# Attention, experts and SwiGLU in one kernel: the order of the first expert's choice, of one weight conversion and of two small tables, and a last tile in halves

## The chip, the cores and the metric

The kernel runs on one core of a Trainium2 chip. The metric is the device time of one launch in microseconds (us), as the median of several runs. A difference of 0.2% is 2.2 us here.

## The reference

Three layers run one after the other on random data:

```python
attn = 1 / (1 + exp(-(q @ k.T / sqrt(64) - log(448))))       # q, k, v: 4 batches, 12 heads, 448 x 64
x    = (attn @ v) as [1792 tokens, 768]
e    = argmax(x @ w_gate)                                     # 8 experts
x    = gate_w * (relu(x @ w1[e]) @ w2[e])                     # 768 -> 1024 -> 768, gate_w a softmax weight
out  = (silu(x @ w2_gate) * (x @ w2_val)) @ w2_out            # 768 -> 1536 -> 768, 64-bit weights
```

## The kernel before

**Attention** walks over 24 pairs of heads, 4 batches of 6 pairs, in a loop written out by hand (`for i, (b, g) in enumerate(pairs)`, from L449). Inside `tc.manual_schedule()` the instructions of every engine stand in the order in which the code issues them, so a line of Python that stands later is queued later on each engine. In iteration i TensorE (PE) computes the scores of pair i+1 in four chunks (`scores`, L214), transposes k and q of pair i+2 (`transpose_qk`, L202), multiplies pair i with v (`av`, L229) and folds pair i-1 (`fold`, L249: it transposes the result back and adds the gate logits of that pair). ScalarE (ACT) makes the sigmoids of the chunks (L226), whose PSUM buffers are two. `load` (L181) fetches q, k and v of pair i+4 on the queue of SyncE (SP).

**Conversion.** The SwiGLU weights are 64-bit numbers. `load_r64` (L137) fetches a block of them, 768 KB, and `convert` (L147) builds 32-bit numbers from their bits in three steps: s0 with one ACT instruction (L152) and one of VectorE (DVE, L153), s1 with one of DVE (L157), s2 with one of DVE (L161) and two of GpSimd (POOL, L163 and L164). One block is converted per pair, its steps between the chunks of the scores, and is stored on POOL's queue (L431). The scratch tile `u` has one buffer.

**Routing.** For each batch, once its six folds are done, a list `tail` gives work to the folds that follow, one item per fold: `gate` (L288), `ranks` with `places` (L300 and L329), and for the third batch also `choose_first` with `first_slot` (L345 and L363), which guess the expert that most tokens chose, and `first_perm` (L379), which finds 128 of its tokens and gathers their rows of x from DRAM (L390). These rows, transposed by `first_x` (L395), meet the guessed expert's weights in `first_product` (L404) while the table of all slots is still being made. The weights of the guess are loaded from L133, w1 in six blocks of 512 KB and w2 in eight of 384 KB.

**The slot table** (L560 to L598) is a run of small DVE instructions. It gives each slot of 128 tokens its expert (`slot_e`), a mark for a new expert (`slot_n`) and its row in the result (`slot_c`). After it the gate weights of the slots, `gsl`, are added up from a PSUM tile `pg` (L596 to L598).

**Experts** (from L907): 19 slots, each with transposed rows, two products, the weights split in a high and a low part (`split_w`, L758). The first matmuls of the stage are transposes into a new PSUM tile (L909), then products with w2 (L921).

**SwiGLU**: `gemm1` (L673) over 12 blocks of columns and four pieces of tokens, then 14 output tiles (L1035 to L1056), each of 72 matmuls into a PSUM tile of two banks, a copy by ACT (L1052) and an indirect store by POOL (L1053) to the tokens' rows.

Of the kernel before, what the change touches and what calls it, by code (L numbers as in the profile page):

```python
# [9 lines left out]
F32 = mybir.dt.float32  # L10
F32R = mybir.dt.float32r
BF16 = mybir.dt.bfloat16
I32 = mybir.dt.int32
U32 = mybir.dt.uint32
AF = mybir.ActivationFunctionType
ALU = mybir.AluOpType
# [6 lines left out]
def sigmoid_attention_moe_swiglu_kernel(  # L23
# [13 lines left out]
    nc = tc.nc  # L37
    B, H, S, D = q.shape
    NT, DM = out.shape
# [3 lines left out]
    P = 128  # L43
# [5 lines left out]
    K2 = F2 // P  # L49
    HH = H // 2  # L50
    HW = DM // 2
    NT_P = NT // P
    NS = (NT + E * (P - 1)) // P
    NSP = NS + (NS % 2)
# [37 lines left out]
    perm_c = const.tile([P, NT_P], I32, name="perm_c")  # L92
# [9 lines left out]
    gsl = const.tile([P, NSP], F32, name="gsl")  # L102
# [65 lines left out]
    with ExitStack() as actx:  # L168
# [12 lines left out]
        def load(nm, i):  # L181
            b, g = pairs[i]
            src = {"q": q, "k": k, "v": v}[nm][b, 2 * g:2 * g + 2]
            if nm == "v":
                t = qkv.tile([CP, 2, C, D], F32, tag=nm, name="vraw", bufs=5)
                nc.sync.dma_start(t, src.rearrange("h (p c) d -> p h c d", c=C))
            else:
                t = qkv.tile([CP, C, 2, D], F32, tag=nm, name=nm + "raw", bufs=4)
                for h in range(2):
                    nc.sync.dma_start(t[:, :, h], src[h].rearrange("(p c) d -> p c d", c=C))  # L190
            raw[nm, i] = t
# [5 lines left out]
        n = len(pairs)  # L197
# [31 lines left out]
        def av(i):  # L229
            vt = raw.pop(("v", i))  # L230
            a = am.pop(i)
            pu = ps_u.tile([P, 512], F32, tag="u", name="pu")
            for c in range(C):
                for h in range(2):
                    nc.tensor.matmul(pu[h * D:(h + 1) * D, :S], vt[:, h, c], a[:, c, h],  # L235
                                     start=(c == 0), stop=(c == C - 1))
            u = up.tile([P, S], F32, tag="u", name="u")
            nc.vector.tensor_copy(u, pu[:, :S])  # L238
            us[i] = u
            qk.pop(("q", i))  # L240
            qk.pop(("k", i))
# [172 lines left out]
        with tc.manual_schedule():  # L414
# [1 line left out]
                for nm in "kqv":  # L416
                    load(nm, i)
            nc.sync.dma_start(fwt[:, :, P:], w_gate.rearrange("(g p) e -> p g e", p=P))
            for i in (2, 3):
                for nm in "kqv":  # L420
                    load(nm, i)
            conv = {}
            cvw = {}

            def load_conv(i):
                r = cvp.tile([P, DM * 2], I32, tag="r64", name="r64", bufs=2)
                load_r64(r, ("gv"[i // K2], i % K2))
                conv[i] = r

            def store_conv(i):  # L430
                nc.gpsimd.dma_start(wgd[i], cvw.pop(i))  # L431

            load_conv(0)
            load_conv(1)
            pw = ps_u.tile([P, 512], F32, tag="u", name="pw")

# [12 lines left out]
            for i, (b, g) in enumerate(pairs):  # L449
                if i + 1 < n:  # L450
                    scores(i + 1, 0)
                    scores(i + 1, 1)
                cvw[i] = cvp.tile([P, DM], F32, tag="w", name="w", bufs=2)
                cv = convert(conv.pop(i), cvp.tile([P, DM], I32, tag="u", name="u", bufs=1),
                             cvw[i])
                if i + 2 < n:
                    transpose_qk(i + 2)
                cv[0]()
                if i + 4 < n:
                    for nm in "kqv":  # L460
                        load(nm, i + 4)
                if i + 1 < n:
                    scores(i + 1, 2)
                    scores(i + 1, 3)
                cv[1]()
                cv[2]()
                store_conv(i)
                if i + 2 < n:
                    load_conv(i + 2)
                av(i)  # L470
                if i > 0:
                    fold(i - 1, tail.pop(0) if tail else None)
                if i == n - 1:
                    first_x()
                if g == 0 and b > 0:
                    tail.append(lambda px, b=b: lambda: gate(b - 1))

                    def rank_place(px, b=b):
                        evac = ranks(b - 1, px)

                        def done():
                            evac()
                            places(b - 1)
                        return done

                    tail.append(rank_place)
                    if b == B - 1:
                        tail.append(lambda px: lambda: (choose_first(B - 2), first_slot()))
                        tail.append(first_perm)
                if i == n - 2:  # L490
                    ge = nc.values_load(guess[0:1, 0:1], engines=[SP], min_val=0, max_val=E - 1,
                                        skip_runtime_bounds_check_because=why)
                    for j in range(KD):
                        load_w(0, j, ge)
                elif i == n - 1:
                    for j in range(3):
                        load_w(1, j, ge)
# [70 lines left out]
            for t in range(T):  # L568
# [5 lines left out]
            se = rp.tile([P, NS, E], F32, tag="se", name="se")  # L574
            V.tensor_tensor(se, iota_s[:, :NS, None].to_broadcast([P, NS, E]),
                            cum.to_broadcast([P, NS, E]), op=ALU.is_ge)
            sf = rp.tile([P, NS], F32, tag="sf", name="sf")
            V.tensor_reduce(sf, se, axis=AX.X, op=ALU.add)
            V.tensor_scalar(sf, sf, float(E - 1), gf, op0=ALU.min, op1=ALU.add)
# [13 lines left out]
            V.tensor_add(sf, sf, iota_p[:, :NS])  # L593
            V.tensor_scalar(slot_c, sf, float(NT), None, op0=ALU.min)

            V.tensor_copy(gsl, pg[:, :NSP])  # L596
            for i in (1, 2):
                V.tensor_add(gsl, pg[:, i * NSP:(i + 1) * NSP], gsl)  # L598

    ectx = ExitStack()  # L600
    early = ectx.enter_context(tc.tile_pool(name="early", bufs=2, side="right", reuse_waits="tile"))
# [297 lines left out]
    with tc.manual_schedule():  # L899
# [135 lines left out]
        for t in range(NT_P):  # L1035
            po = ps_a.tile([P, 2, 512], F32, tag="a", name="po")
            hh, hl = hs.pop(t)
            for f in range(K2):
                for st, mv, i in ((hh, 0, 0), (hh, 1, 1), (hl, 0, 2)):
                    for m in range(2):  # L1040
                        nc.tensor.matmul(po[:, m, :HW], st[:, f],  # L1041
                                         wo[f][mv][:, m * HW:(m + 1) * HW],
                                         start=(f == 0 and i == 0),
                                         stop=(f == K2 - 1 and i == 2))
            if t + 2 < NT_P:
                split_h(t + 2)
                for f in range(KS, K2):
                    split_hb(t + 2, f)
                if t + 3 < NT_P:
                    load_h(t + 3)  # L1050
            ob = post.tile([P, DM], F32, tag="ob", name="ob", bufs=2)
            nc.scalar.copy(ob.rearrange("p (m f) -> p m f", m=2), po[:, :, :HW])  # L1052
            nc.gpsimd.indirect_dma_start(  # L1053
                out=out[:, :],
                out_offset=bass.IndirectOffsetOnAxis(ap=perm_c[:, t:t + 1], axis=0),
                in_=ob[:, :], in_offset=None)  # L1056
# [31 lines left out]
```

## Time and profile before

| | |
|---|---|
| median of 3 runs | 1124.3 us (1124.15 to 1124.78) |
| the profiled execution | 1125.06 us, span 1123.5 us |
| TensorE (PE) | 1093.8 us busy, 97% of the span |
| VectorE (DVE) | 627.9 us, 56% |
| ScalarE (ACT) | 531.7 us, 47% |
| GpSimd (POOL) | 277.1 us, 25% |
| DMA | 168.17 MB, mean 150 GB/s |

The profiled execution took 1.56 us more than its span and 0.76 us more than the median. In the lists of the profile an instruction is named by its line, engine, operation and tiles; a bracket behind it tells how long its engine sat idle before it and what ended that. PE is busy nearly throughout, so what counts is where it is idle and what clock it was granted (a clock of 1.00 is 2.4 GHz, 0.50 is 1.2 GHz).

### The profile page before, as it was taken

To read this page: it belongs to the slowest core of one execution; us is meant where nothing else is said; L and a number is where in the kernel's file an instruction comes from. 1 tells how busy PE (TensorE), PEld (TensorE's weight loads), DVE (VectorE), ACT (ScalarE), POOL (GpSimd) and SP (SyncE) were. 2 spreads that over 40 slices of the span, in tenths; PEclk is the share of its full clock that TensorE was granted. 3 is DMA by queue.
4 is the path that set the end of the run, shared out by engine and by line. 5 is a ranking of instruction groups with operands and counts; after the bars stand their busy time and mean duration, and the time that the engine had idled before them with its cause. 6 is when DMAs were issued, how large, how long until landed. Compare 5 with 4: busy or idle time off the path is not lost. (4 is left out here: it accounts for less than half of the span.)

```text
span 1123.5 us, 16847 instructions
## 1 busy us (share of the span) xinstructions
PE 1093.8 (97%) x6130; PEld 913.7 (81%) x6130; DVE 627.9 (56%) x918; ACT 531.7 (47%) x720; POOL 277.1 (25%) x241
## 2 busy tenths in 40 slices
PE   7999999789999999999999999999999999999996
PEld 5565655468989798989888888888888889999996
DVE  3667777569899999999954333333333335111210
ACT  5666676248889788888852211111111124111210
POOL 2555556422222422223101011111111110000100
PEclk9999999889999999999999999999999999999998
DMA  8898987722445883644322232222222324322220
GB/s 208 240 272 247 273 250 214 282 99 85 159 152 183 299 321 125 214 153 169 127 96 99 86 112 103 104 103 103 104 104 104 113 94 137 105 83 76 75 89 29
DMA packets 124278, 168.17 MB, mean 150 GB/s; under 512 B 50592, under 2 KB 94112, under 8 KB 124192
## 3 DMA queue, kind: packets, MB, share of 16 engines
q1 hardware_dynamic: 118112, 137.16, 38.3%
q0 software_dynamic: 6080, 29.90, 7.3%
q8 instruction: 50, 0.82, 0.3%
q14 instruction: 36, 0.29, 0.1%
HBM read 195.98 MB, written 41.82 MB: 212 GB/s over the span
## 5 line engine op out<-in xcount | busy, mean ns | idle before, releaser
L687 PE MATMUL psf<-y,wgh 128*128 128x512 f32 (+1 forms) x1152 | 322.9, 367 | 0.2 <-ACTq L944 0.2
L765 DVE TENSOR_TENSOR wlo<-wraw,whi 128x768 fp32r<-128x768 f32 (+1 forms) x256 | 271.1, 1108 | 29.3 <-ACT whi L763 27.6
L763 ACT CAST whi<-wraw 128x768 fp32r<-128x768 f32 (+1 forms) x256 | 230.2, 929 | 51.7 <-PE hps L787 32.4
L687 PEld LDWEIGHTS psf<-y,wgh 128*128 128x128 f32 x1152 | 205.1, 188 | 36.6 <-ACTq L944 0.5
L687 PE MATMUL psf<-y,wgl 128*128 128x512 f32 (+1 forms) x576 | 210.5, 365 | 0.0
L163 POOL TENSOR_SCALAR w<-w 128x768 f32<-128x768 f32 x36 | 84.7, 2354 | 312.3 <-ACT w L152 312.3
L692 ACT ACTIVATE sg<-psf 128x512 f32<-128x512 f32 (+1 forms) x48 | 26.1, 544 | 250.0 <-PE psf L687 250.0
L1041 PE MATMUL po<-y,hh 128*128 128x384 f32 x672 | 144.1, 335 | 0.0
L693 DVE TENSOR_TENSOR sg<-psf,sg 128x512 f32<-128x512 f32 (+1 forms) x48 | 30.0, 625 | 194.6 <-ACT sg L692 194.6
L687 PEld LDWEIGHTS psf<-y,wgl 128*128 128x128 f32 x576 | 108.3, 188 | 18.8
L226 ACT ACTIVATE a<-sc,logs 112x896 f32<-112x896 f32 x96 | 91.9, 1015 | 58.9 <-PE sc L224 58.7
L1041 PEld LDWEIGHTS po<-y,hh 128*128 128x128 f32 x672 | 119.3, 188 | 0.0
L75 DVE TENSOR_TENSOR hl<-ht,hh 128x1280 fp32r<-128x1280 f32 x14 | 20.9, 1491 | 125.1 <-ACT hh L74 125.1
L1041 PE MATMUL po<-y,hl 128*128 128x384 f32 x336 | 85.6, 335 | 0.0
L235 PE MATMUL pu<-a,vraw 112*64 112x448 f32 x384 | 77.5, 545 | 0.4 <-DVE u L238 0.4
L787 PE MATMUL yps<-whi,hh 128*128 128x384 f32 x296 | 77.2, 341 | 0.0
L787 PE MATMUL yps<-wlo,hh 128*128 128x384 f32 x296 | 75.9, 337 | 0.8 <-DVE wlo L765 0.8
L787 PE MATMUL yps<-whi,hl 128*128 128x384 f32 x296 | 75.4, 335 | 0.0
L74 ACT CAST hh<-ht 128x1280 fp32r<-128x1280 f32 x14 | 17.7, 1265 | 120.0 <-PE po L1041 120.0
L164 POOL TENSOR_TENSOR w<-w,u 128x768 f32<-128x768 f32 x36 | 66.6, 1849 | 29.6 <-DVE u L161 29.3
L787 PE MATMUL hps<-whi,xh 128*128 128x512 f32 x216 | 68.4, 397 | 0.0
L787 PE MATMUL hps<-wlo,xh 128*128 128x512 f32 x216 | 67.3, 393 | 1.1 <-DVE wlo L765 1.1
(189 smaller groups left out, 1494.8 us busy)
## 6 DMA issues: line engine op xcount, KB each, us to landing
wraw<-in_moe_w_dram SPq DMA_DIRECT2D x148, 384.0 KB
wraw<-in_moe_w_dram SPq DMA_DIRECT2D x108, 512.0 KB
r<-in_moe_w_gate_dram SPq DMA_DIRECT2D x12, 768.0 KB
wgd<-w POOLq DMA_DIRECT2D x24, 384.0 KB, 5.6
r<-in_moe_w_val_dram SPq DMA_DIRECT2D x12, 768.0 KB
w<-wgd SPq DMA_DIRECT2D x24, 384.0 KB
r<-in_moe_w_out_dram SPq DMA_DIRECT2D x12, 768.0 KB
ht<-hd SPq DMA_DIRECT2D x14, 640.0 KB
```

The costliest lines, as they stand in the source:

```text
L75: nc.vector.tensor_sub(lo, src, hi.bitcast(F32))
L163: nc.gpsimd.tensor_scalar(w, w, TINY, None, op0=ALU.is_ge)
L164: nc.gpsimd.tensor_tensor(w, w, u.bitcast(F32), op=ALU.mult)
L226: nc.scalar.activation(am[i][:, c], sc[:CP, :, :S], AF.Sigmoid, bias=logs[:CP], scale=SCALE)
L235: nc.tensor.matmul(pu[h * D:(h + 1) * D, :S], vt[:, h, c], a[:, c, h], start=(c == 0), stop=(c == C - 1))
L687: nc.tensor.matmul(ps[:, i, :cn], st[:, a], mv[:, j, :cn], start=(j == 0 and m == 0), stop=(j == KD - 1 and m == 2))
L692: nc.scalar.activation(sg[:, :cn], ps[:, 0, :cn], AF.Sigmoid)
L693: nc.vector.tensor_mul(sg[:, :cn], ps[:, 0, :cn], sg[:, :cn])
L763: nc.scalar.copy(hi[:, :w], r)
L765: nc.vector.tensor_sub(lo[:, :w0], r[:, :w0], hi[:, :w0].bitcast(F32))
L787: nc.tensor.matmul(ps[:, m, :w], st[:, a], mv[:, m * w:(m + 1) * w], start=(j == 0 and i == 0), stop=(j == m_ - 1 and i == 2))
L1041: nc.tensor.matmul(po[:, m, :HW], st[:, f], wo[f][mv][:, m * HW:(m + 1) * HW], start=(f == 0 and i == 0), stop=(f == K2 - 1 and i == 2))
```

## The change

Five moves. (1) `load_conv(0)` stands ahead of the loads of pair 3 instead of behind them. (2) In iteration 0 the whole conversion stands behind `av(0)`; in the others it stays where it was. In all of them `load_conv(i + 2)` stands behind `av(i)`; it issues on SP alone, where `av` has nothing. (3) The items of `tail` are appended ahead of the fold of the same iteration, so each item runs with the fold before the one it ran with. (4) `gsl` is added up ahead of the rest of the slot table. (5) The last output tile is computed column half by column half; each half is copied and stored by itself, with indices `perm_h` into rows of half length.

```diff
@@ -416,9 +416,8 @@
                 for nm in "kqv":
                     load(nm, i)
             nc.sync.dma_start(fwt[:, :, P:], w_gate.rearrange("(g p) e -> p g e", p=P))
-            for i in (2, 3):
-                for nm in "kqv":
-                    load(nm, i)
+            for nm in "kqv":
+                load(nm, 2)
             conv = {}
             cvw = {}
 
@@ -431,6 +430,8 @@
                 nc.gpsimd.dma_start(wgd[i], cvw.pop(i))
 
             load_conv(0)
+            for nm in "kqv":
+                load(nm, 3)
             load_conv(1)
             pw = ps_u.tile([P, 512], F32, tag="u", name="pw")
 
@@ -455,38 +456,44 @@
                              cvw[i])
                 if i + 2 < n:
                     transpose_qk(i + 2)
-                cv[0]()
+                if i > 0:
+                    cv[0]()
                 if i + 4 < n:
                     for nm in "kqv":
                         load(nm, i + 4)
                 if i + 1 < n:
                     scores(i + 1, 2)
                     scores(i + 1, 3)
-                cv[1]()
-                cv[2]()
-                store_conv(i)
+                if i > 0:
+                    cv[1]()
+                    cv[2]()
+                    store_conv(i)
+                av(i)
+                if i == 0:
+                    for f in cv:
+                        f()
+                    store_conv(i)
                 if i + 2 < n:
                     load_conv(i + 2)
-                av(i)
+                if g == 0 and b > 0:
+                    tail.append(lambda px, b=b: lambda: gate(b - 1))
+
+                    def rank_place(px, b=b):
+                        evac = ranks(b - 1, px)
+
+                        def done():
+                            evac()
+                            places(b - 1)
+                        return done
+
+                    tail.append(rank_place)
+                    if b == B - 1:
+                        tail.append(lambda px: lambda: (choose_first(B - 2), first_slot()))
+                        tail.append(first_perm)
                 if i > 0:
                     fold(i - 1, tail.pop(0) if tail else None)
                 if i == n - 1:
                     first_x()
-                if g == 0 and b > 0:
-                    tail.append(lambda px, b=b: lambda: gate(b - 1))
-
-                    def rank_place(px, b=b):
-                        evac = ranks(b - 1, px)
-
-                        def done():
-                            evac()
-                            places(b - 1)
-                        return done
-
-                    tail.append(rank_place)
-                    if b == B - 1:
-                        tail.append(lambda px: lambda: (choose_first(B - 2), first_slot()))
-                        tail.append(first_perm)
                 if i == n - 2:
                     ge = nc.values_load(guess[0:1, 0:1], engines=[SP], min_val=0, max_val=E - 1,
                                         skip_runtime_bounds_check_because=why)
@@ -574,6 +581,9 @@
             se = rp.tile([P, NS, E], F32, tag="se", name="se")
             V.tensor_tensor(se, iota_s[:, :NS, None].to_broadcast([P, NS, E]),
                             cum.to_broadcast([P, NS, E]), op=ALU.is_ge)
+            V.tensor_copy(gsl, pg[:, :NSP])
+            for i in (1, 2):
+                V.tensor_add(gsl, pg[:, i * NSP:(i + 1) * NSP], gsl)
             sf = rp.tile([P, NS], F32, tag="sf", name="sf")
             V.tensor_reduce(sf, se, axis=AX.X, op=ALU.add)
             V.tensor_scalar(sf, sf, float(E - 1), gf, op0=ALU.min, op1=ALU.add)
@@ -593,9 +603,6 @@
             V.tensor_add(sf, sf, iota_p[:, :NS])
             V.tensor_scalar(slot_c, sf, float(NT), None, op0=ALU.min)
 
-            V.tensor_copy(gsl, pg[:, :NSP])
-            for i in (1, 2):
-                V.tensor_add(gsl, pg[:, i * NSP:(i + 1) * NSP], gsl)
 
     ectx = ExitStack()
     early = ectx.enter_context(tc.tile_pool(name="early", bufs=2, side="right", reuse_waits="tile"))
@@ -1035,13 +1042,29 @@
         for t in range(NT_P):
             po = ps_a.tile([P, 2, 512], F32, tag="a", name="po")
             hh, hl = hs.pop(t)
-            for f in range(K2):
-                for st, mv, i in ((hh, 0, 0), (hh, 1, 1), (hl, 0, 2)):
-                    for m in range(2):
-                        nc.tensor.matmul(po[:, m, :HW], st[:, f],
-                                         wo[f][mv][:, m * HW:(m + 1) * HW],
-                                         start=(f == 0 and i == 0),
-                                         stop=(f == K2 - 1 and i == 2))
+            last = t == NT_P - 1
+            order = [(f, x, m) for f in range(K2) for x in range(3) for m in range(2)]
+            if last:
+                order.sort(key=lambda a: a[2])
+                ob = post.tile([P, DM], F32, tag="ob", name="ob", bufs=2)
+            for f, x, m in order:
+                st, mv = ((hh, 0), (hh, 1), (hl, 0))[x]
+                nc.tensor.matmul(po[:, m, :HW], st[:, f], wo[f][mv][:, m * HW:(m + 1) * HW],
+                                 start=(f == 0 and x == 0), stop=(f == K2 - 1 and x == 2))
+                if last and f == K2 - 1 and x == 2:
+                    ms = slice(m * HW, (m + 1) * HW)
+                    nc.scalar.copy(ob[:, ms], po[:, m, :HW])
+                    nc.gpsimd.indirect_dma_start(
+                        out=out.rearrange("n (h c) -> (n h) c", h=2),
+                        out_offset=bass.IndirectOffsetOnAxis(ap=perm_h[:, m:m + 1], axis=0),
+                        in_=ob[:, ms], in_offset=None)
+            if last:
+                break
+            if t == 0:
+                perm_h = post.tile([P, 2], I32, tag="permh", name="permh", bufs=1)
+                for m in range(2):
+                    nc.vector.tensor_scalar(perm_h[:, m:m + 1], perm_c[:, NT_P - 1:], 1, m,
+                                            op0=ALU.logical_shift_left, op1=ALU.bitwise_or)
             if t + 2 < NT_P:
                 split_h(t + 2)
                 for f in range(KS, K2):
```

On ACT, at the start (`a_307` the sigmoids of pair 1, `a_388` those of pair 2, `qh` the high part of q, `w_324` of the first conversion). Before, and then now:

```order
L74 CAST qh_340<-pq_335 128x448
L152 ACTIVATE w_324<-r64_184 128x768
L226 ACTIVATE a_307<-sc_354,logs_72 112x896
L226 ACTIVATE a_307<-sc_362,logs_72 112x896
L226 ACTIVATE a_388<-sc_389,logs_72 112x896
```

```order
L74 CAST qh_340<-pq_335 128x448
L226 ACTIVATE a_307<-sc_352,logs_72 112x896
L226 ACTIVATE a_307<-sc_360,logs_72 112x896
L152 ACTIVATE w_324<-r64_176 128x768
L226 ACTIVATE a_388<-sc_389,logs_72 112x896
```

The conversion's ACT instruction stood ahead of the last two sigmoids of pair 1; it now stands behind them.

On POOL, at the end of attention (`wgd` is where a converted block is stored, `rot` to `oh0` belong to the choice of the first slot, `x0` is its gather). Before, and then now:

```order
L431 DMA wgd_64<-w_2330 128x768
L353 TENSOR_SCALAR rot_147<-iota_e_91,gf_86 128x8
...
L375 TENSOR_TENSOR oh0_2416<-tok2_101,z_2411 112x24
L163 TENSOR_SCALAR w_2435<-w_2435 128x768
...
L431 DMA wgd_64<-w_2435 128x768
L390 DMA x0_2497<-xd_60,perm0_85 128x768
L163 TENSOR_SCALAR w_2508<-w_2508 128x768
...
L431 DMA wgd_64<-w_2508 128x768
L716 DMA xg_2740<-xd_60,perm_g_76 128x768
```

```order
L430 DMA wgd_64<-w_2247 128x768
L353 TENSOR_SCALAR rot_147<-iota_e_91,gf_86 128x8
...
L375 TENSOR_TENSOR oh0_2333<-tok2_101,z_2328 112x24
L163 TENSOR_SCALAR w_2352<-w_2352 128x768
...
L430 DMA wgd_64<-w_2352 128x768
L390 DMA x0_2433<-xd_60,perm0_85 128x768
L163 TENSOR_SCALAR w_2452<-w_2452 128x768
...
L163 TENSOR_SCALAR w_2508<-w_2508 128x768
...
L723 DMA xg_2740<-xd_60,perm_g_76 128x768
```

The choice and the gather each stand one conversion earlier: two conversions now follow the gather ahead of `xg`, where one did.

On DVE, the slot table (`se`, `sf` the sums of which it is made, `pg` the PSUM tile of the gate weights). Before, and then now:

```order
L575 TENSOR_TENSOR se<-iota_s,cum 128x168
L578 TENSOR_REDUCE sf<-se 128x21
...
L594 TENSOR_SCALAR slot_c<-sf 128x21
L596 COPY gsl<-pg 128x22
L598 TENSOR_TENSOR gsl<-pg,gsl 128x22 x2
```

```order
L582 TENSOR_TENSOR se<-iota_s,cum 128x168
L584 COPY gsl<-pg 128x22
L586 TENSOR_TENSOR gsl<-pg,gsl 128x22 x2
L588 TENSOR_REDUCE sf<-se 128x21
...
L604 TENSOR_SCALAR slot_c<-sf 128x21
```

The last reads of `pg` now stand ahead of 13 instructions of the table instead of behind them.

## Rows read from the trace of the kernel before

**Rows 1.** Windows: us, busy us by engine (instructions), PEclk, DMA share, GB/s.

```profile
60.00:200.00 140.00, 139.38 (x988) 81.47 (x988) 103.74 (x223) 94.72 (x124) 83.09 (x61) 1.00 0.87 251
...
300.00:590.00 290.00, 287.54 (x1553) 260.85 (x1553) 262.77 (x286) 244.60 (x316) 74.36 (x84) 1.00 0.54 185
```

**Rows 2.** Waits, engine PE: total us, times, longest us.

```profile
PE pt L400 <- DMA x<-xd,perm: 7.2, 1, 7.2
...
PE pt L909 <- DVE gsl L598: 3.2, 1, 3.2
```

**Rows 3.** Timeline of PE, first pairs: start us, us, instructions [idle before].

```profile
16.83 3.23 PE L235 MATMUL pu<-a,vraw 112*64 112x448 f32 x16
23.10 0.46 PE L224 MATMUL sc<-qh,kh 64*112 64x448 f32 x2 [3.04 <-ACT a L226]
```

**Rows 4.** Timeline of ACT, the same stretch.

```profile
21.24 0.91 ACT L152 ACTIVATE w<-r 128x768 f32<-128x768 f32 x1 [4.75 <-DMA r<-in_moe_w_gate_dram]
22.06 4.00 ACT L226 ACTIVATE a<-sc,logs 112x896 f32<-112x896 f32 x4
```

**Rows 5.** Timeline of PE, from the last fold but one to the experts.

```profile
205.97 1.18 PE L259 MATMUL px<-fwt,u 128*112 128x136 f32 x8
214.31 1.51 PE L400 MATMUL pt<-ident,x 128*128 128x128 f32 x6 [7.17 <-DMA x<-xd,perm]
...
217.70 2.59 PE L408 MATMUL hps<-wraw,x0t 128*128 128x512 f32 x4
...
220.44 7.11 PE L408 MATMUL hps<-wraw,x0t 128*128 128x512 f32 x16
...
229.89 0.72 PE L569 MATMUL pg<-oh,ohl 112*128 112x66 bf16 x16
233.80 1.94 PE L909 MATMUL pt<-ident,hsb 128*128 128x128 f32 x8 [3.18 <-DVE gsl L598]
```

**Rows 6.** Windows, columns as in the first group: where the clock was low.

```profile
24.00:28.00 4.00, 4.00 (x22) 3.03 (x24) 2.15 (x5) 3.71 (x5) 3.41 (x3) 0.57 0.93 255
...
208.00:212.00 4.00, 0.00 (x0) 0.00 (x0) 0.89 (x5) 0.00 (x0) 3.62 (x3) 1.00 0.93 336
214.30:220.00 5.70, 5.68 (x18) 4.04 (x19) 1.86 (x9) 2.55 (x4) 0.00 (x0) 0.58 0.98 383
233.80:240.00 6.20, 6.20 (x16) 4.03 (x17) 3.51 (x5) 4.10 (x6) 0.00 (x0) 0.53 0.07 30
```

**Rows 7.** Timeline of POOL, end of attention.

```profile
195.73 0.59 POOL L431 DMA_DIRECT2D wgd<-w  x1 [0.30 <-POOL w L164]
...
205.93 1.22 POOL L390 DMA_INDIRECT x<-xd,perm  x1 [0.40 <-issue]
```

**Rows 8.** Tiles x and xg: gathers from issue to landing.

```profile
DMA to landing us min/median/max: 8.2/8.2/8.2
...
DMA to landing us min/median/max: 3.8/4.1/4.6
```

**Rows 9.** Timeline of SP's queue, the loads of the guessed expert.

```profile
203.44 0.58 SPq L278 DMA_DIRECT2D xd<-xt  x1
205.41 7.33 SPq L133 DMA_DIRECT2D wraw<-in_moe_w_dram  x9
```

**Rows 10.** Timeline of DVE, last fold but one and end of the slot table.

```profile
208.40 0.16 DVE L268 COPY lp<-px 112x8 f32<-112x8 f32 x1
...
230.31 0.33 DVE L578 TENSOR_REDUCE sf<-se 128x21 f32<-128x168 f32 x1
...
233.25 0.40 DVE L598 TENSOR_TENSOR gsl<-pg,gsl 128x22 f32<-128x22 f32 x2
```

**Rows 11.** The last store: its copy, a half-width copy elsewhere, GB/s by 0.2 us.

```profile
1114.30 0.80 ACT L1052 COPY ob<-po 128x768 f32<-128x768 f32 x1 [11.75 <-PE po L1041]
...
L402 ACT COPY x0t<-pt x2: 479/479/479, 215.2 to 215.9; 128x384 f32<-128x384 f32 x2
...
GB/s 0 0 0 0 0 0 0 0 0 399 307 307 461 461 31 0 0 0 0 0 0 0 0 0 0 0 0 0 0 0 0 0 0 0 0 0 0 0 0 0
```

More of the change, by code (lines that the diff above doesn't have):

```diff
@@ L464, in sigmoid_attention_moe_swiglu_kernel @@
                     scores(i + 1, 3)
-                cv[1]()
-                cv[2]()
-                store_conv(i)
+                if i > 0:
[7 more added lines that the diff above has]
+                    store_conv(i)
                 if i + 2 < n:
                     load_conv(i + 2)
-                av(i)
[L471 to L474, printed above, removed]
                 if g == 0 and b > 0:
@@ L489, in sigmoid_attention_moe_swiglu_kernel @@
                         tail.append(first_perm)
+                if i > 0:
+                    fold(i - 1, tail.pop(0) if tail else None)
+                if i == n - 1:
+                    first_x()
                 if i == n - 2:
```

## The prediction, before the changed kernel was run

> **What bounds the kernel now.** I read the windows first. PE is busy for 139.38 of the 140 us of steady attention and for 287.54 of 290 us of the experts [rows 1], at a clock of 1.00 in both. So no engine beside PE sets the pace there, and what the change can earn lies in the few places where PE stands still or runs at half clock. The list of PE's waits gives two large ones, 7.2 us for the gathered rows of the first slot and 3.2 us for the gate weights [rows 2]; the timeline of the first pairs adds a third, 3.04 us behind a sigmoid [rows 3]. Then the windows behind these three waits: after each, the granted clock falls to the lower level of 1.2 GHz for some microseconds in which PE has work. Time lost is length times (1 - PEclk): 4.00 us at 0.57, so 1.72 us; 5.70 us at 0.58, so 2.39 us; 6.20 us at 0.53, so 2.91 us [rows 6].
>
> So the three stalls cost 3.04 + 7.17 + 3.18 = 13.39 us idle [rows 3, 5] and 7.02 us of slow clock, 20.4 us in all. That is the ceiling of the first four moves.
>
> **Start, moves 1 and 2.** ACT sat 4.75 us, from 16.49 to 21.24, in front of the first conversion's instruction, whose 768 KB block had not landed; the sigmoids queued behind it held the two PSUM buffers of the scores, so PE could not begin pair 2 until 23.10 [rows 3, 4]. In the new order those sigmoids run from about 16.5 to 18.4 (four took 4.00 us), before PE ends its product with v at 20.06. The wait goes, and the slow clock behind it: 3.04 + 1.72 = 4.76 us. What is late next? Pair 3's loads now queue behind the block; their transposes come at about 21.4. The trace has no row for their landing. Bound: the block landed at 21.24 with pair 3 ahead of it, so block and pair 3 in either order are there by then at the latest, if the following block does not overtake. That is just in time, so I charge nothing for it and keep 2.5 us as the far end. The first conversion on DVE now ends about when pair 3's parts are split, so its scratch tile frees late, the second conversion is late, and the copy that frees the fold's PSUM buffers with it: I take 0.5 us, between 0 and 1.1. Gain **4.2 us**, between 2.2 and 4.8.
>
> **First slot, move 3.** Today the chain of the choice starts on POOL at 196.3, behind the store of 195.73, and the gather is issued at 205.93, when the last weights' store and nine loads of the guessed expert enter the same DMA engines; it needs 8.2 us to land. Gathers in a quiet stretch need 3.8 to 4.6 us [rows 7, 8]. A pair has 56 matmuls (24 for scores, 8 transposes, 16 with v, 8 of the fold) and 988 ran in 140 us [rows 1], so one conversion earlier is about 8 us. The gather is then issued near 198.5 and lands near 203, before PE ends the last fold but one at 207.14. So the 7.17 us go, with 2.39 us of slow clock: 9.56 us. Against that stand two new waits. First, the second half of the transposes needs the PSUM buffer of that fold, which DVE frees with the copies that end at 208.56 [rows 10], while PE would be there at 207.5 (207.14 and half of the 1.51 us at double speed); DVE is hardly earlier than before. 1.0 us, between 0.5 and 1.3. Second, the products with w1 would start near 209.8 instead of 217.70 (less 7.17 and 1.7 of slow clock until there, plus 1.0), but its loads do not start earlier: SP issues them behind the store of x at 203.44 and the read of the guess, the first at 205.41 [rows 9], and both hang on the fold's copies on DVE. Ahead of the first block (0.52 MB) stand that store (0.92 MB) and one converted block (0.39 MB): 1.83 MB. At 336 GB/s [rows 6] that is 5.4 us, from about 204.5, and the queue starts slowly: I take 210.5. PE then takes a block in 4 x 444 = 1.78 us (7.11 us for 16 matmuls [rows 5]), the DMA brings one in 0.52 MB / 0.383 MB per us = 1.4 us [rows 6], and the later ones are in time. 0.7 us, between 0 and 2.6 (the last of the nine loads was issued at about 212.4 [rows 9]; I expect the first to be there by then). Gain **7.9 us**, between 5.8 and 9.1. The choice's work on POOL and DVE, one pair earlier, only delays a conversion that nobody on PE waits for.
>
> **Gate weights, move 4.** PE ends the product for `pg` at 230.61 and waits for the last of the three `gsl` instructions until 233.80, because the transposes take over that PSUM buffer [rows 5, 10]. In the new order they run right behind `se`, which ends near the same time (the next instruction starts at 230.31): one copy and two instructions that took 0.40 us [rows 10], some 0.8 us with the handover. Idle saved 3.18 - 0.8 = 2.4 us; slow clock 2.91 us; at full clock PE reaches the product with w2 before ACT has the first transposes copied, 0.4 us of new wait. The table itself ends 0.6 us later in its own order, but its readers, SP's reads and the first weight loads, come only with the first weight conversions, behind these transposes. Gain **4.9 us**, between 1.5 (the clock still falls) and 5.3.
>
> **Last tile, move 5.** The first half leaves while PE computes the second. At the end stand a copy of half width, 0.48 for 0.80 us, and half of a transfer that now takes about 1.0 us [rows 11]: 0.32 + 0.5 = **0.8 us**, between 0.3 and 1.2. The matmul count is the same, and the two index instructions on DVE stand in the first output tile.
>
> **Sum.** 4.2 + 7.9 + 4.9 + 0.8 = 17.8 us. The profiled execution of 1125.06 would become 1107.3; it stands 0.76 above the median, so for the median 1124.3 - 17.8 = **1106.5 us**.
>
> **Rivals.**
> - *The weights take the gather's place.* If the first block of w1 lands only at 212.4, PE waits 2.6 instead of 0.7 us, and the stretch with so little work lets the clock fall again, 2.39 us. 17.8 - 1.9 - 2.4 = 13.5, so 1110.8. For it: the loads start no earlier, and DMA is at 0.93 of its engines [rows 6]. Against it: 0.39 MB of gather are out of the way.
> - *The clock stays low at the experts' start.* PE still has two short gaps (0.8 and 0.4 us) between small matmuls and transposes, and gets 2.91 us back only if the higher level holds: 1109.4. The three falls each followed an idle stretch of 3 us or more [rows 3, 5], which speaks against it. The Trainium skill, "TensorE: Matmul & The Clock Gate", section "A second HAM failure mode: psum-queue depth-cycling", says that frequent short gaps between groups of matmuls can also make the clock swing; no row here shows such a case. By that rule this rival would be the forecast.
> - *The start pays little.* Pair 3 comes some 2.5 us late behind the big block, with 1.7 us of slow clock: 13.6 us remain, 1110.7.
> - *Move 4 does nothing*, because the transposes wait for something else that ends with the table, for instance another buffer: 17.8 - 4.9, so 1111.4. The list of waits names `gsl` [rows 2], which speaks against it.
> - *Slower than before.* The chain of the conversions (DVE, POOL, DVE, one scratch tile) becomes the pace of attention once it has been pushed late at pair 0 and at the choice, and never catches up. It decides if the chain takes over 8 us a pair; with 22 pairs and 0.95 us more on each the time would be 1124.3 - 17.8 + 20.9 = 1127.4. DVE is busy 103.74 of 140 us and POOL 83.09 [rows 1], so both have slack to catch up.
>
> **How the numbers follow.** Forecast (all moves pay, 1104.5 to 1108.5) 0.50, weights late 0.18, clock low 0.14, start poor 0.10, move 4 empty 0.04, slower 0.02, and 0.02 for no measurable difference (within 0.2%, 2.2 us, about what a measurement of this kernel can tell from none). All others are faster: 0.96. For the range I go down to 1104.3 (ceiling of 21.2 us with the smallest new waits, 1.2 us, and noise) and up to 1111.8, which takes in each single rival on the fast side; two of them together, or slower, are the 2 in 10 left out.
>
> **What would show it.** Right: no wait of PE over 1 us between 10 and 240 us; the conversion's first ACT instruction behind four sigmoids with no idle in front of them; the gather issued before 200 less the start's gain, landing within 5 us; the transposes of the first slot within 1 us of the product for `pg`; PEclk 1.00 in all three windows. Wrong: PE waiting for `wraw` or for `kraw` and `qraw`, a slow clock behind `pg`, or attention's windows with PE below 0.98.

## The result, and the profile after

The changed kernel takes **1110.93 us** in the median of 4 runs (1109.78 to 1112.21), beside 1124.49 us for the kernel before (1124.15 to 1124.78). The ratio is 0.988, with a 95% interval of 0.9863 to 0.9897: 13.6 us off, where 17.8 were forecast. The profiled execution took 1112.21 us with a span of 1110.6, so 12.85 us less than that of before. It is the slowest of the four and has the lowest mean granted clock, 0.994 beside 0.996 to 0.997.

What PE waits for now, in the list of waits (total us, times, longest), beside [rows 2]:

```profile
PE pt L400 <- DVE lp L268: 1.6, 1, 1.6
PE hps L408 <- DMA wraw<-in_moe_w_dram: 1.5, 1, 1.5
PE sc L224 <- ACT a L226: 1.4, 2, 0.8
...
PE pt L916 <- DVE gsl L586: 0.8, 1, 0.8
...
PE po L1052 <- ACT ob L1056: 0.6, 1, 0.6
...
PE yps L928 <- ACT hT L920: 0.2, 1, 0.2
```

The 7.2 and 3.2 us are gone. In their place stand 1.6 us for a PSUM buffer and 1.5 us for w1 at the first slot, 0.8 us for the gate weights, and a wait that is new, 0.6 us in the last output tile (L1052).

The timeline of PE (start us, us, instructions, [idle before]) at the places of [rows 3, 5]:

```profile
16.53 3.23 PE L235 MATMUL pu<-a,vraw 112*64 112x448 f32 x16
...
23.41 3.23 PE L235 MATMUL pu<-a,vraw 112*64 112x448 f32 x16
29.86 0.58 PE L207 MATMUL pq<-ident,qraw 112*128 112x112 f32 x4 [0.17 <-PE pk L207]
31.78 3.23 PE L235 MATMUL pu<-a,vraw 112*64 112x448 f32 x16
...
197.51 3.23 PE L235 MATMUL pu<-a,vraw 112*64 112x448 f32 x16
200.66 1.18 PE L259 MATMUL px<-fwt,u 128*112 128x136 f32 x8
201.68 0.49 PE L400 MATMUL pt<-ident,x 128*128 128x128 f32 x3
203.79 0.52 PE L400 MATMUL pt<-ident,x 128*128 128x128 f32 x3 [1.62 <-DVE lp L268]
204.14 1.09 PE L259 MATMUL px<-fwt,u 128*112 128x136 f32 x8
206.69 3.78 PE L408 MATMUL hps<-wraw,x0t 128*128 128x512 f32 x4 [1.45 <-DMA wraw<-in_moe_w_dram]
...
221.20 0.72 PE L576 MATMUL pg<-oh,ohl 112*128 112x66 bf16 x16
222.72 1.07 PE L916 MATMUL pt<-ident,hsb 128*128 128x128 f32 x8 [0.80 <-DVE gsl L586]
...
229.29 0.82 PE L735 MATMUL pt<-ident,xg 128*128 128x128 f32 x6
```

Three lines of the kernel before that belong beside these, the products of pairs 2 and 23 with v and the first transposes of the second slot's rows:

```profile
36.65 3.23 PE L235 MATMUL pu<-a,vraw 112*64 112x448 f32 x16
...
202.81 3.23 PE L235 MATMUL pu<-a,vraw 112*64 112x448 f32 x16 [0.39 <-DVE u L238]
...
242.81 0.82 PE L728 MATMUL pt<-ident,xg 128*128 128x128 f32 x6
```

The windows behind the three former stalls, columns as in [rows 6]:

```profile
24.00:28.00 4.00, 4.00 (x28) 1.98 (x24) 3.20 (x4) 2.21 (x3) 3.64 (x3) 1.00 1.12 296
...
206.00:212.00 6.00, 5.32 (x14) 2.55 (x15) 1.90 (x10) 0.43 (x2) 0.00 (x0) 0.50 1.01 369
...
214.30:220.00 5.70, 5.70 (x29) 2.83 (x28) 3.44 (x14) 0.00 (x0) 0.00 (x0) 1.00 1.05 407
221.00:224.00 3.00, 1.98 (x25) 1.47 (x24) 2.35 (x15) 1.70 (x4) 1.61 (x2) 1.00 0.92 317
```

The clock no longer falls at the start or behind the gate weights, but it still falls in the middle: from 206 to about 212.6 us PE computes the first products with w1 at 1.2 GHz. Four of them take 3.78 us there; at full clock, in the kernel before, 16 took 7.11 us [rows 5]. Six us at half speed are 3.0 us lost, the microsecond behind them (0.64) adds 0.4, and 0.35 go off for the time in which PE was idle anyway: about 3.1 us in this execution.

Place by place, against the kernel before: pair 2's product with v starts at 31.78 instead of 36.65 us, **4.9 us** earlier (0.3 of them are there already at pair 0's, 16.53 instead of 16.83, ahead of anything that the moves change), and pair 23's at 197.51 instead of 202.81; from there to the product for `pg` it is 23.69 instead of 27.08 us, so the first slot gains 3.4 and, with the 0.4 us between pairs 2 and 23, **3.8 us**; from `pg` to the first transposes of the second slot's rows 8.09 instead of 12.92 us, **4.8 us**. That is 13.5 us. The experts and the products behind them keep it, and the end gives back **0.6 us**:

```profile
1094.15 0.34 PE L1052 MATMUL po<-y,hl 128*128 128x384 f32 x1
1095.10 0.62 PE L1052 MATMUL po<-y,hh 128*128 128x384 f32 x2 [0.61 <-ACT ob L1056]
```

Here PE has ended the first half of the last tile and waits until ACT has copied it, though the second half goes to the other bank. In the timeline of ACT the two copies start 7.12 us apart:

```profile
1088.29 0.80 ACT L1075 COPY ob<-po 128x768 f32<-128x768 f32 x1 [10.58 <-issue]
1094.57 0.48 ACT L1056 COPY ob<-po 128x384 f32<-128x384 f32 x1 [5.48 <-PE po L1052]
1101.69 0.48 ACT L1056 COPY ob<-po 128x384 f32<-128x384 f32 x1 [6.64 <-PE po L1052]
```

Three questions follow. Is each part worth what the trace says, by itself? Is the wait for w1 what brings the clock down (theory A), or the 1.62 us ahead of it, for the copies of DVE (theory B)? And does the last tile lose because its halves share a PSUM tile?

### The profile page after: what moved, and what is told of

Same layout as the page of the kernel before. It is cut to its first block, busy times and chain, and to the rows that moved or that the text cites. A ratio compares the mean times of both kernels' runs of the same rounds, so it can differ in the third digit from the quotient of the medians.

```text
span 1110.6 us, 16852 instructions
## 1 busy us (share of the span) xinstructions
PE 1090.6 (98%) x6130; PEld 910.5 (82%) x6130; DVE 628.2 (57%) x920; ACT 531.9 (48%) x721; POOL 276.8 (25%) x242
## 5 line engine op out<-in xcount | busy, mean ns | idle before, releaser
L1052 PE MATMUL po<-y,hh 128*128 128x384 f32 x672 | 146.2, 336 | 0.6 <-ACT ob L1056 0.6
L1052 PEld LDWEIGHTS po<-y,hh 128*128 128x128 f32 x672 | 119.4, 188 | 0.9 <-ACT ob L1056 0.9
L1052 PE MATMUL po<-y,hl 128*128 128x384 f32 x336 | 87.5, 335 | 0.0
```

Of the source, the lines that this page charges most:

```text
L1052: nc.tensor.matmul(po[:, m, :HW], st[:, f], wo[f][mv][:, m * HW:(m + 1) * HW], start=(f == 0 and x == 0), stop=(f == K2 - 1 and x == 2))
```

## Experiments

Each run has runs of the kernel before beside it on the same chip. A gain in us is one minus the ratio, times that median of before.

| run | median us | ratio to before (95%) | gain us |
|---|---|---|---|
| start alone (moves 1, 2) | 1119.92 | 0.9966 (0.9955 to 0.9977) | 3.8 |
| pair 3's loads alone (move 1) | 1119.98 | 0.9961 (0.9948 to 0.9974) | 4.4 |
| first conversion alone (move 2) | 1121.91 | 0.9981 (0.9969 to 0.9992) | 2.1 |
| first slot alone (move 3) | 1119.23 | 0.9958 (0.9943 to 0.9973) | 4.7 |
| gate weights alone (move 4) | 1119.12 | 0.9960 (0.9948 to 0.9972) | 4.5 |
| changed, last tile whole | 1110.62 | 0.9887 (0.9869 to 0.9905) | 12.7 |
| changed, two PSUM tiles | 1111.60 | 0.9888 (0.9869 to 0.9907) | 12.6 |
| changed, rows' own PSUM | 1111.80 | 0.9898 (0.9881 to 0.9916) | 11.5 |
| the same again | 1110.71 | 0.9884 (0.9860 to 0.9907) | 13.0 |
| changed, w1 early | 1108.20 | 0.9871 (0.9852 to 0.9889) | 14.5 |
| w1 early, longer copies | 1107.64 | 0.9850 (0.9831 to 0.9869) | 16.9 |
| w1 early and two PSUM tiles | 1106.98 | 0.9853 (0.9833 to 0.9874) | 16.5 |

### The parts one by one

**Start alone.** The kernel before with `load_conv(0)` ahead of pair 3's loads and the first conversion behind `av(0)`.

> The kernel before with the first two moves alone (pair 3's loads behind the first weight block, the first conversion behind pair 0's product with v). The prediction gave them 4.2 us, with 0.5 us for a late conversion chain. The trace of the changed kernel shows pair 1's product with v 5.2 us earlier and pair 23's 5.3 us earlier, so I expect 5.0 to 5.3 us off the time of before, and later waits (7.2 us for the gathered rows, 3.2 us for the gate weights) unchanged in length.

Gain 3.8 us (2.6 to 5.1), under the 5.0 to 5.3 expected, and close to the prediction's 4.2. In its profile pair 1's product with v starts at 23.81 us instead of 28.64, but 0.54 us are lost again at pair 4's transposes, and pair 23's starts at 198.71, 4.1 us earlier than before:

```profile
23.81 3.23 PE L235 MATMUL pu<-a,vraw 112*64 112x448 f32 x16
30.63 0.57 PE L207 MATMUL pq<-ident,qraw 112*128 112x112 f32 x4 [0.54 <-PE pk L207]
...
198.71 3.23 PE L235 MATMUL pu<-a,vraw 112*64 112x448 f32 x16 [0.38 <-DVE u L238]
...
210.26 1.51 PE L400 MATMUL pt<-ident,x 128*128 128x128 f32 x6 [7.21 <-DMA x<-xd,perm]
```

That wait near 30 us is what is late next; the profile does not name what ends it. It was 0.17 us in the profile of the changed kernel and 1.07 in that of the two PSUM tiles.

**Which of the two moves.** Two runs with one of them each (parts of their diffs; the first also takes pair 3's loads out of the loop further up):

```diff
...
             load_conv(0)
+            for nm in "kqv":
+                load(nm, 3)
             load_conv(1)
```

> The kernel before with pair 3's loads behind the first weight block, and nothing else. The block then lands some 2.5 us earlier, ACT is held less long in front of the first conversion, and I expect 2 to 3 us off the time of before; if pair 3's own loads then come late at its transposes, nothing is gained.

```diff
+                if i > 0:
-                cv[0]()
+                    cv[0]()
...
                 av(i)
+                if i == 0:
+                    for f in cv:
+                        f()
```

> The kernel before with the first conversion behind pair 0's product with v, and nothing else. The sigmoids no longer stand behind the block's landing at about 21 us. If that order alone is what earns the start, this has all of it, 3.8 us; if the block's late landing then holds the conversion in front of pair 2's sigmoids instead, 1 to 2 us.

The loads alone earn 4.4 us (2.9 to 5.8), at least as much as both moves; the conversion alone 2.1 (0.9 to 3.5). With the loads moved, ACT waits 1.96 instead of 4.75 us [rows 4] for the block, which now lands at 18.61 us, and PE stands still for only 0.28 us:

```profile
18.61 0.94 ACT L152 ACTIVATE w<-r 128x768 f32<-128x768 f32 x1 [1.96 <-DMA r<-in_moe_w_gate_dram]
```

So the order of the loads is what pays; no gain of move 2 on top of it can be measured.

**First slot alone.** The kernel before with the items of `tail` appended ahead of the fold of the same iteration, for every batch.

> The kernel before with the third move alone (the choice of the first slot one fold earlier). The prediction gave it 7.9 us. Theory A (w1 takes the place of the gathered rows: 1.5 to 2.5 us of wait, and the clock falls behind it): 3.4 us off the time, as between the two traces from pair 23's product with v to the product for the gate weights (8.7 us in all, less 5.3). Theory B (the wait for w1 alone is the loss and the clock is a matter of chance): 5 to 7 us off.

Gain 4.7 us (3.0 to 6.4): the prediction's 7.9 lies outside, theory A's 3.4 inside, and so does the lower part of the 5 to 7 us of this run's theory B, by which the clock is a matter of chance; the time does not decide between them. The same two waits are there, 1.66 and 1.72 us, and behind them the clock falls (window 210 to 216 us of this kernel):

```profile
210.00:216.00 6.00, 4.91 (x13) 2.33 (x14) 1.64 (x11) 0.57 (x2) 0.00 (x0) 0.52 1.02 374
```

**Gate weights alone.** The three `gsl` instructions behind `se`, nothing else.

> The kernel before with the fourth move alone (gate weights ahead of the slot table). The prediction gave it 4.9 us: 2.4 us of idle, 2.9 us of slow clock, less 0.4 us. If the trace of the changed kernel can be split by place, 4.8 us off the time of before and PEclk 1.00 behind the gate weights. Rival: alone, behind the 7.2 us stall that is still there, the clock falls behind the shorter wait as well, and only 2 us are gained.

Gain 4.5 us (3.1 to 5.8), as predicted (4.9). The wait is 0.80 us also behind the stall of 7.15 us that this kernel still has, and the clock behind it is 1.00 (0.53 before [rows 6]):

```profile
230.00:238.00 8.00, 6.96 (x41) 4.57 (x41) 7.22 (x24) 5.08 (x8) 1.52 (x2) 1.00 0.34 98
```

The three parts together make 13.0 us, the whole change 13.6; with intervals of over 1 us on each part that is no difference.

### What brings the clock down at the first slot

**w1 early.** The changed kernel with

```diff
-                if i == n - 2:
+                if i == n - 3:
                     ge = nc.values_load(guess[0:1, 0:1], ...
...
-                elif i == n - 1:
+                elif i == n - 2:
                     for j in range(3):
```

> The changed kernel with the guess read and the six blocks of w1 issued on SP one pair earlier, ahead of the first store of x instead of behind it. Theory A (the first block of w1 is what PE now waits for, and the slow clock comes from the thin work while it waits): the 1.45 us before the first product with w1 go, the clock stays at 1.00 there, the 5 blocks take 9 us instead of 11.8, and the time falls by about 4 us, to 1106.5 to 1107.5. Theory B (the clock falls because of the 1.62 us between the two groups of transposes, behind DVE's copies, whatever the weights do): the 1.45 us go, the clock still falls, and the time falls by 1 to 1.5 us. Rival C: the loads now run beside the gather of the first slot's rows, which lands late as it did before (8.2 us), and the wait moves there: same or slower than 1110.9.

In the profile both waits shrink, 1.45 to nothing and 1.62 to 0.55 us (the latter because DVE, whose copies PE waits for, got through its conversion 1 us sooner; see the last section), and the clock holds (window 206 to 212 us). Timeline of PE, and windows:

```profile
203.14 0.52 PE L400 MATMUL pt<-ident,x 128*128 128x128 f32 x3 [0.55 <-DVE lp L268]
203.50 1.09 PE L259 MATMUL px<-fwt,u 128*112 128x136 f32 x8
204.42 1.88 PE L408 MATMUL hps<-wraw,x0t 128*128 128x512 f32 x4
...
206.81 7.11 PE L408 MATMUL hps<-wraw,x0t 128*128 128x512 f32 x16
```

```profile
206.00:212.00 6.00, 5.82 (x21) 2.69 (x21) 5.05 (x23) 0.10 (x1) 0.47 (x1) 1.00 1.04 409
```

From pair 23's product with v to the first transposes of the second slot it takes 26.5 us where the changed kernel took 31.8 (197.93 to 224.41, 197.51 to 229.29). The profiled run is the fastest of its four, and by the medians' ratios the gain over the changed kernel is 1.0 us, over the run with the last tile whole, on the same chip, 1.8: less than the 4 expected, and neither is clear of the noise. Rival C is out: the gather now takes 8.1 us, as before [rows 8], but it is issued at 193.79, and so lands just in time. Both waits went in this run, though, so it does not tell theory A from B.

**The rows in a PSUM tile of their own.** `first_x` takes one tile of the scores' pool in place of two of `ps_t`, w1 as in the change:

```diff
+            pt2 = ps_s.tile([P, 2, 512], F32, tag="sc", name="pt0")
             for j0 in range(0, KD, 3):
-                pt = ps_t.tile([P, 512], F32, tag="tr", name="pt0")
+                pt = pt2[:, j0 // 3]
```

> The changed kernel with the transposes of the first slot's rows in a PSUM tile of the scores' pool, so that the second group does not wait for DVE's copies of the fold; the loads of w1 as they are. Theory A: the 1.62 us go from there, the wait for w1 becomes longer by what PE comes earlier (0.5 to 1.6 us), the clock still falls, time within 0.5 us of 1110.9. Theory B: without the first gap the clock holds, and the time falls by 2 to 3 us, to about 1108.5.

> The kernel of the run with the rows' own PSUM tile once more, for a second profile of a single wait of 2.6 us for w1 with no gap of over 0.6 us ahead of it. If one wait of that length alone doesn't bring the clock down, PEclk is 1.00 from 200 to 220 us again; if it was chance, the clock falls this time behind the wait, and PE's 16 products take about 8 us instead of 7.2.

The wait for w1 grew to 2.63 us in the first profile and 2.78 in the second, with only 0.57 us ahead of it, and in both **the clock held at 1.00**. PE in the second, and its window:

```profile
204.00 0.55 PE L401 MATMUL pt<-ident,x 128*128 128x128 f32 x3 [0.57 <-ACT x0t L403]
204.39 1.10 PE L259 MATMUL px<-fwt,u 128*112 128x136 f32 x8
208.27 1.98 PE L409 MATMUL hps<-wraw,x0t 128*128 128x512 f32 x4 [2.78 <-DMA wraw<-in_moe_w_dram]
```

```profile
208.00:214.00 6.00, 5.73 (x20) 2.61 (x21) 3.15 (x17) 0.00 (x0) 0.00 (x0) 1.00 1.01 386
```

So theory A, as put, does not stand: one wait for w1 of 2.63 or 2.78 us did not bring the clock down. In all four profiles with about 1.6 us, a short piece of work, and then 1.45 to 2.4 us (the change, the first slot alone, and both runs on the last tile) it fell. Yet neither median is better than that of the changed kernel, against theory B's 2 to 3 us. In the profiles the stretch from pair 23's product with v to the second slot's rows did become shorter, 28.4 and 28.5 us beside 31.8, but pair 23's product came 1.4 and 1.3 us later, behind waits at the start, and both profiled runs are the fastest of their four. The granted clock of the single runs calls for care too: it lies between 0.994 and 0.998, and at 0.996 or less in 4 of these 8 runs, though both profiled runs have 0.998. So some runs lose clock, and no profile shows where.

**w1 early, with the 1.6 us put back.**

```diff
             gs = slice(g * P, (g + 1) * P)
+            if i == n - 2:
+                for _ in range(2):
+                    nc.vector.tensor_copy(xt[b][:, :C3, gs], pv[:, :, :P])
```

> The changed kernel with w1 one pair earlier, and DVE's first copy of the last fold but one made three times instead of once (0.56 us each, same data), so that PE again waits about 1.6 us between the two groups of transposes while w1 is there in time. It separates the two gaps, which both went in the run with early weights. Theory A (w1's wait is what brings the clock down): PEclk stays 1.00 from 200 to 220 us and the time is 1 us above that run, about 1109. Theory B (the 1.6 us gap brings it down): the clock is at its lower level after it, and the time is 3 to 4 us above, 1111 to 1112. Both gaps needed, one after the other: as theory A.

This missed its aim. With the longer copies the buffers were handed out in another order: the second group of transposes and the fold behind it wait for ACT's copies of the first slot's rows, 0.57 us each, and no gap of 1.6 us came about.

```profile
203.22 0.55 PE L403 MATMUL pt<-ident,x 128*128 128x128 f32 x3 [0.57 <-ACT x0t L405]
204.34 1.18 PE L259 MATMUL px<-fwt,u 128*112 128x136 f32 x8 [0.57 <-ACT x0t L405]
205.35 1.88 PE L411 MATMUL hps<-wraw,x0t 128*128 128x512 f32 x4
```

The clock held, and the time is 1107.64 us in spite of the added work. The other order also cut the wait for the gate weights to 0.18 us. Whether the gap of 1.6 us alone brings the clock down stays open.

What the runs together do show: in the 13 runs with w1 early (three kernels) the granted clock was 0.997 or 0.998 every time; in the 22 runs with moves 1 to 4 and w1 late (the change, the two on the last tile below, the rows' own PSUM twice) it was 0.996 or less in 9. So **with w1 early the mean clock was high in every run, and with w1 late it was low in some runs only**; where the runs without a profile lost it, and which of the gaps in front of the products decides, is open.

### The last tile

Two edits of the changed kernel: `last = False`, so that the tile is stored whole, and a second PSUM tile for the second half:

```diff
             last = t == NT_P - 1
+            po2 = [po, ps_a.tile([P, 2, 512], F32, tag="a", name="po") if last else po]
...
```

> The changed kernel with the last output tile whole again, as before. The prediction gave the halves 0.8 us, so by it this runs 0.8 us longer, 1111.7. By the trace (from the last matmul of the experts to the end of the span 185.1 us before and 185.6 to 185.8 us now) the halves cost 0.5 us, so this runs at about 1110.4.

> The changed kernel with the two halves of the last output tile in two PSUM tiles, so that the second half's matmuls need not wait for the copy of the first. If the shared tile is the cost, the 0.61 us wait of PE goes and the time falls by 0.6 us, to 1110.3. If the end is set by the landing of the second store alone, nothing changes, 1110.9.

The medians (1110.62 and 1111.60) cannot tell them apart. The traces can, since the end repeats to within 0.1 us: from the start of the copy of the last tile but one to the end of the span it is 22.3 us with the halves (in the change, with w1 early, and with the rows' own PSUM), 21.7 whole (before and here), and 21.4 with two tiles (21.5 with w1 early besides). ACT's copies with two tiles, and POOL's last store of the whole tile:

```profile
1096.64 0.48 ACT L1057 COPY ob<-po 128x384 f32<-128x384 f32 x1 [5.48 <-PE po L1053]
1102.88 0.48 ACT L1057 COPY ob<-po 128x384 f32<-128x384 f32 x1 [5.76 <-PE po L1053]
```

```profile
1101.90 0.96 POOL L1076 DMA_INDIRECT out_dram<-ob,perm_c  x1 [11.59 <-ACT ob L1075]
```

With two tiles the copies start 6.24 us apart instead of 7.12, so the shared tile costs 0.9 us. What is left of the gain is 0.3 us, all of it the shorter copy. The smaller store gives nothing: from its issue to the end of the span 8.10 us whole (span 1110.0) and 8.16 in halves (1102.44, 1110.6), although the half lands in 2.6 instead of 3.0 us.

### Both together

w1 early and the second PSUM tile in one kernel.

> The changed kernel with w1 one pair earlier and the last halves in two PSUM tiles, the two edits that the runs so far speak for. By the traces: 5.0 us for the weights (product with w2 at 219.1 instead of 224.0) and 0.9 us for the two tiles (22.3 us from the last but one copy to the end of the span with one tile, 21.4 with two), so 1105 to 1107 in the middle of its runs, about 1.5% below before. If the weights' gain was one lucky run, 1109.

1106.98 us, all four runs between 1106.58 and 1107.55, where the changed kernel's lay between 1109.78 and 1112.21. This version, and the one with w1 early and longer copies, beat the kernel before by 16.5 to 17 us; the intervals of their ratios still overlap a little with that of the changed kernel. From the run with two PSUM tiles this kernel differs by w1 alone, and by the two ratios that is worth 3.9 us, the 4 that were expected of w1 early; these intervals, too, overlap by a little. Its first transposes of the gathered rows start at 203.18 us, some 0.2 us behind the fold; the gather, issued at 194.69, needed 8.4. It is the next wait there.

## Why the prediction was right, and where it was not

The time lies inside the range and the sign is right; the forecast of 1106.5 is 4.4 us too low. Step by step, against the profiled execution:

- **Start**: 4.2 forecast, 4.9 in the trace (4.6 counted from pair 0's product with v), 3.8 (2.6 to 5.1) alone. Right, by the mechanism given: the sigmoids run at once, the 4.75 us of ACT [rows 4] become 0.63, as the timeline of ACT after the change has it. The 0.5 us for a late conversion chain did not come; a wait at pair 4's transposes, 0.17 us here and 0.54 alone, took part of it instead. The step did not see that the loads alone would do.

```profile
18.61 0.92 ACT L152 ACTIVATE w<-r 128x768 f32<-128x768 f32 x1 [0.63 <-DMA r<-in_moe_w_gate_dram]
```

- **First slot**: 7.9 forecast, 3.8 in the trace, 4.7 (3.0 to 6.4) alone. **This is the step that failed, in the size of its two new waits and in a slow clock put at nothing.** The 7.17 us went, as said, and the gather landed in 4.6 us. But the PSUM buffer cost 1.62 instead of 1.0 us (ahead of the copies that free it a conversion step of DVE took 2.00 us instead of 0.96, see the last section), the first block of w1 1.45 instead of 0.7 (it came some 6.6 us behind its issue at 200.12, not 5.1; SP's line stands below), and the clock, charged with nothing, cost 3.1. These are 4.5 us. A wait of 0.4 us ahead of pair 23's product with v went besides, uncounted. The argument that the clock falls only behind 3 us of idleness, drawn from three cases, was too weak: two waits of about 1.5 us with 1.4 us of work between them were followed by a fall too, though not in every run. The low end of the step's range, 5.8 us, held no slow clock (its own terms give 5.7: 9.56 less 1.3 and 2.6), and the gain in the trace lies below it. A wait for `wraw` stood on the prediction's own list of signs of being wrong; of its three windows two have a clock of 1.00.

```profile
200.12 6.97 SPq L133 DMA_DIRECT2D wraw<-in_moe_w_dram  x9
```

- **Gate weights**: 4.9 forecast, 4.8 in the trace, 4.5 (3.1 to 5.8) alone. Right in each term: 0.80 us of wait left, clock at 1.00, 0.24 us for `hT` (0.4 forecast).
- **Last tile**: 0.8 forecast, 0.6 lost. Wrong sign. The copy is shorter, as said, but the shorter store gives nothing, and that PE would compute the second half "while" the first leaves was not so: both halves lie in one PSUM tile, and the matmuls of the second waited for the copy of the first.

The rivals: *the weights take the gather's place* gave 1110.8 and comes nearest. Its mechanism is what the trace shows, with a shorter wait (1.45 for 2.6 us) and a longer slow stretch (3.1 for 2.4 us); that the total fits as well is in part luck, since the start gave 0.7 us more than forecast and the last tile 1.4 less. I held it at 0.18, since 0.39 MB of gather were out of the way; the step that should have raised it is my own remark that the loads start no earlier. *Clock low at the experts' start* did not come: 1.00 in the window from 221 us, 0.53 before [rows 6]. The page of the Trainium skill cited with it ("TensorE: Matmul & The Clock Gate", section "A second HAM failure mode: psum-queue depth-cycling"), says that frequent short idle times between groups of matmuls can make the clock swing. At the place where the prediction put it the trace does not agree: 1.00. At the first slot, 15 us earlier, the clock fell once, to 0.50, behind gaps of 1.62 and 1.45 us, but it held at 1.00 behind 0.57 and 2.78 us; no run here shows a swing between the levels from frequent gaps. *Start poor*, *move 4 empty* and *slower* are excluded by the runs of the parts.

## What to carry to other kernels

When a wait is taken away, ask of the next operand not only when it is needed but what issues it: here w1's loads hung on a store and a read that had not moved, and moving them one pair earlier brought the time to 1108.2 us, and to 1107.0 with a second PSUM tile at the end, where 1106.5 were forecast. A short wait may not be cheap if another stands close before it: in four profiles of four such a pair was followed by the slow clock, so a step's range should hold its price. Here an output split in halves overlapped fully only when each half had its own tile, and half a store at the end did not end the kernel earlier.

## What was unexpected of the hardware

- One idle stretch of PE of 2.63 and 2.78 us left the clock at 1.00 in both profiles, while 1.62 and 1.45 us with 1.4 us of work between were followed by the lower level in the profile of the change. The sum of the gaps does not tell the cases apart: 0.57 us stood ahead of the long ones, so 3.20 and 3.35 us held and 3.07 us fell. Between runs of one kernel the mean granted clock varies (0.994 to 0.997 for the change, with 1112.21 us at the lowest and 1109.78 at the highest).
- DVE's second step of the last conversion took 2.00 us in the changed kernel, beside a POOL instruction, and 0.96 us with w1 early, where POOL started 1.6 us later; its copies, and PE behind them, came that much later. The six profiles with the third move and w1 late all have 2.00 us for this step, the three with w1 early 0.96; that the POOL instruction beside it is the cause was not tested. The timelines of DVE and of POOL of the changed kernel:

```profile
199.34 2.00 DVE L157 SCALAR_TENSOR_TENSOR u<-r,u 128x768 int32<-128x768 int32 x1
...
203.54 0.16 DVE L268 COPY lp<-px 112x8 f32<-112x8 f32 x1
```

```profile
199.68 2.16 POOL L163 TENSOR_SCALAR w<-w 128x768 f32<-128x768 f32 x1
```
